# Windowed attention and two gated MLPs: decoded weights kept in HBM for the second half of the tokens

## The chip, the cores and the metric

One Trainium2 chip, one of its cores. The metric is the device time of one execution in microseconds (us). The core's engines work side by side and wait for one another through semaphores: PE (TensorE, matrix products; its weight loads are a row of their own, PEld), DVE (VectorE), ACT (ScalarE), POOL (GpSimd), and SP (SyncE), whose queue issues every DMA of this kernel in the order in which the DMAs stand there.

## What is computed

Attention over 4 sequences of 576 tokens, 8 heads of 64, each query seeing the 64 latest keys; its output, 2304 tokens by 512, goes through two gated MLPs with a hidden width of 1536:

```
x = attention(q, k, v)                                   # 2304 x 512
x = ((x @ w_val) / (1 + exp(-(x @ w_gate)))) @ w_out
x = ((x @ w_a) * (x @ w_b)) @ w_out2
```

The six weight matrices come as float64, everything else as float32.

## The kernel before

Tokens are worked in nine blocks of 256, in two halves (line 32): blocks 0 to 4, then blocks 5 to 8. A half goes through attention, then the first MLP ("phase 0"), then the second ("phase 1"). Blocks share a pass in groups of up to two, so that most products over the model dimension have 512 columns. The hidden width is cut into 12 chunks of 128, and a chunk needs three weight matrices of 128 x 512, here "a", "b" and "o". Both MLPs have 24 chunks, both halves 48 (`NW`, line 412), numbered F.

Weights reach the PE as pairs of float32r numbers, a high part and the rest, that sum to the float32 value. `load_weights` (line 237) fetches a chunk's float64 words, 512 KB a matrix, into one of three staging tiles. `decode` (line 251) makes the pair: ACT scales the low word (L259), DVE picks exponent and mantissa apart and together (L262, L266, L269, L274), POOL adds the low word (L272), ACT rounds to the high part (L279, wah/wbh/woh), POOL subtracts it to get the rest (L280, wal/wbl/wol). That is four DVE, two POOL and two ACT instructions a matrix, 144 matrices. Each half decodes all 24 chunks; the second half decodes the same words again. The pool `wts` has G + 1 = 4 places for each part, so that chunk F takes the place of chunk F - 4.

On the PE, `product` (L293) makes the gate sum gps and the value sum vps, 12 matmuls each (four chunks of the model dimension by three pairs of parts). `hidden` turns them into hh and hl (L307 to L316). `project` (L332) multiplies with "o" into acc, and `evacuate` (L349, L351) adds acc to the block's sum xacc. After the last chunk of phase 0 the sum becomes the input of phase 1: ACT writes its high part xh (L356), POOL the rest xl (L357).

Phases are cut into turns, each a group of blocks with up to three chunks; a group's projections are put out during the next turn. `step_decode` (line 416) moves the decoding on by a matrix, twice for every hidden chunk of a two-block group, once the place is free (`last_use`). The order in which each engine gets its instructions is then made by the framework's scheduler; each engine, and SP's queue, runs it in order.

Of the kernel before, what the change touches and what calls it, by code (L numbers as in the profile page):

```python
# [10 lines left out]
I32 = mybir.dt.int32  # L11
# [8 lines left out]
def tile_window_attention_gated_mlps(ctx, tc, q, k, v, w1g, w1v, w1o, w2a, w2b, w2o, out):  # L20
# [4 lines left out]
    P = 128  # L25
    NP = H // 2            # head pairs = chunks of the model dimension
    NF = DFF // P          # chunks of the hidden dimension
    G = 3                  # hidden chunks whose products are summed in PSUM
    N = 256                # tokens of a block
    TB = N // P            # 128-token tiles of a block  # L30
    # blocks that share their products over the model dimension, in two halves
    HALVES = (((0,), (1, 2), (3, 4)), ((5, 6), (7, 8)))
    W = 2 * N
    LAG = 1                # steps between the starts of two units of attention
    WIN = 64
    KW = P + WIN           # keys that a 128-query tile can see
    QSCALE = -1.0 / float(D) ** 0.5    # scores are kept negated
    MASKED = 1.0e30
# [12 lines left out]
    work = ctx.enter_context(tc.tile_pool(name="work", bufs=3))  # L51
    small = ctx.enter_context(tc.tile_pool(name="small", bufs=5))
    ps_acc = ctx.enter_context(tc.tile_pool(name="ps_acc", bufs=2, space=PSUM))
    ps_gv = ctx.enter_context(tc.tile_pool(name="ps_gv", bufs=3, space=PSUM))
    ps_at = ctx.enter_context(tc.tile_pool(name="ps_at", bufs=3, space=PSUM))
    ident = const.tile([P, P], F32, name="ident")
    make_identity(nc, ident)
    # the tensor engine's clock is up by the time that the first rows are here
    warm = ps_gv.tile([P, P], F32, tag="gv", name="warm")
    for _ in range(7):  # L60
        nc.tensor.matmul(warm, lhsT=ident, rhs=ident, start=True, stop=True)
    # queries in halves of 64, each with its window of 128 keys; the rows are those of two heads.
    # key c of the window, WIN - c tokens before the half's first query, is open to query p for
    # p + 1 <= c <= p + WIN
    mask_n = const.tile([P, P], F32, name="mask_n")
    mask_0 = const.tile([P, P], F32, name="mask_0")
    nc.gpsimd.memset(mask_n, 0.0)
    for e in range(2):
# [8 lines left out]
        )  # L77
    # the first half of a sequence has no keys before it
    nc.vector.tensor_copy(mask_0, mask_n)
    nc.vector.memset(mask_0[:, 0:WIN], MASKED)  # L80

    # ---------------------------------------------------------------- attention
    lo, hi = slice(0, D), slice(D, P)
    before, own, last = slice(0, WIN), slice(WIN, KW), slice(P, KW)
    prev = {}
    # columns: pair of heads, half of the queries, head of the pair, query; Q of the even heads
    # above zeros, of the odd heads below zeros
    qts = [const.tile([P, 2, 2, 2, WIN], F32, name=f"qt{i}") for i in range(3)]
# [12 lines left out]
    def attention(t, hq, xhi, xlo, c0):  # L101
        """Tokens [128 t, 128 t + 128) of heads [4 hq, 4 hq + 4); the result, split, goes to columns
        c0... of xhi, xlo. A generator: it stops where other work may come between."""
        starts = [j for j in range(2) if (t * P + j * WIN) % S == 0]
# [7 lines left out]

        # keys' window of the transposed K, two heads to a column; scores are kept negated
        # the first units have the banks to themselves
        p_kq, p_s = (ps_acc, "acc") if t < 4 else (ps_at, "at"), (ps_gv, "gv") if t < 2 else (ps_at, "at")
# [16 lines left out]
        prev["k", hq] = kt  # L132
        # V of the 64 keys before the tile and of its first half
        vb = work.tile([P, 4, D], F32, tag="vb", name=f"vb{t}_{hq}")
# [55 lines left out]

    # places of x: the result of the first MLP follows its input, and each group of the second
    # half one of the first half
    PLACE = {(0,): 0, (1, 2): 1, (3, 4): 2, (5, 6): 3, (7, 8): 1}
    x, done = {}, set()

    def new_x(phase, group):
        """Tiles for x of a group, in parts that sum to it; blocks have their slices."""
        w = len(group) * N
        place = PLACE[group]
        x[phase, group] = pair = tuple(  # L200
            xs.tile([P, NP, w], F32R, tag=f"x{p}{place}", name=f"x{p}{phase}_{group[0]}") for p in "hl"
        )
        for i, b in enumerate(group):
            x[phase, (b,)] = tuple(t[:, :, i * N:(i + 1) * N] for t in pair)
# [10 lines left out]
    def attention_stream(blocks):  # L215
        """The units of the blocks, a new one under way every LAG steps."""
        units = (u for blk in blocks for u in attention_units(blk))
# [13 lines left out]

    # ------------------------------------------------------------------ weights
    mats = ((w1g, w1v, w1o), (w2a, w2b, w2o))
    words = [[w.bitcast(I32) for w in m] for m in mats]    # float64: low word, high word
    staged, ready = {}, {}

# [14 lines left out]
    def decode(F):  # L251
        """Hidden chunk's weights: float64 words to float32 (rounded at the 24th bit) and on to
        float32r pairs that sum to it exactly. A generator, one matrix at a time."""
        got = {}
        for nm in "abo":
# [3 lines left out]
            nc.scalar.activation(out=low, in_=w0.bitcast(U32), func=AF.Copy, scale=2.0 ** -29)  # L259
            # the exponent: what lies below float32's range becomes 0  # L260
            ex = dec.tile([P, DM], I32, tag="ex", name="ex")
# [14 lines left out]
            )  # L276
            wh = wts.tile([P, DM], F32R, tag=f"w{nm}h", name=f"w{nm}h")
            wl = wts.tile([P, DM], F32R, tag=f"w{nm}l", name=f"w{nm}l")
            nc.scalar.activation(out=wh, in_=wf, func=AF.Copy)  # L279
            nc.gpsimd.tensor_tensor(out=wl, in0=wf, in1=wh.bitcast(F32), op=ALU.subtract)  # L280
            got[nm] = (wh, wl)
            yield
        ready[F] = got

    # --------------------------------------------------------------------- MLPs
    def product(ps, w, x):
        """ps = w^T x over the model dimension; the product of the two rests is below what the
        sums keep."""
        (wh, wl), (xh, xl) = w, x
        n = 0  # L290
        for c in range(NP):
            for a, b in ((wh, xh), (wh, xl), (wl, xh)):
                nc.tensor.matmul(  # L293
                    ps, lhsT=a[:, c * P:(c + 1) * P], rhs=b[:, c, :], start=(n == 0), stop=(n == 3 * NP - 1)
                )
                n += 1

    def hidden(phase, w, x):
# [6 lines left out]
        if phase == 0:  # L305
            # the logistic function is (1 + tanh(x / 2)) / 2; tanh is in one table set with exp
            nc.scalar.activation(out=hr, in_=gps, func=AF.Tanh, scale=0.5)  # L307
# [13 lines left out]
    def project(phase, acc, w, h, begin, end):  # L321
# [7 lines left out]
        for m, ps in enumerate(outs):  # L329
            for n, (a, b) in enumerate(pairs):  # L330
                # a start clears the written bits of the whole bank: one for both of its sums
                nc.tensor.matmul(  # L332
# [7 lines left out]
    def evacuate(phase, blk, acc, begin, end):  # L340
        """Adds the products of a few hidden chunks to what the block has so far."""
        if begin:
# [18 lines left out]

    # The turns of a phase: a block and the hidden chunks it takes. They are staggered, so that
    # chunks are done with, and others are needed, one at a time.
    # the first turns, and before each what is to be ready: blocks of attention, chunks of weights
    FIRST = (
# [8 lines left out]
    def turns(order, half, ph):  # L374
# [10 lines left out]

        if (half, ph) == (0, 0):     # as blocks come in one by one
            for _, b, fcs in FIRST:
                take((b,), len(fcs))
        elif ph == 0:
            for g in order:  # L390
                for b in g:
                    take((b,), G)
# [23 lines left out]
    def step_decode(turn):  # L416
        """One matrix of the next chunk, if the place for it is free in this turn."""
        if dec_it[0] is None:
            F = ndec[0]
            if F >= NW or (F > G and last_use[F - G - 1] >= turn):  # L420
                return False
            if nload[0] <= F:
                load_weights(F)
                nload[0] = F + 1
            dec_it[0] = decode(F)
            ndec[0] += 1
        if next(dec_it[0], "done") == "done":
            dec_it[0] = None
            F = ndec[0]
            if F < NW and nload[0] <= F:  # L430
                load_weights(F)
# [10 lines left out]
    def attend(blk=None, steps=0):  # L442
        """Puts out attention up to the end of a block, or so many steps of it."""
        while (blk is not None and blk not in done) or steps > 0:
# [11 lines left out]
    for n, (half, ph, group, fcs) in enumerate(plan):  # L456
# [14 lines left out]
        for i, fc in enumerate(fcs):  # L471
# [3 lines left out]
            if (half, ph) == (0, 1) and fc == NF - 1 and PLACE[group] == PLACE[HALVES[1][1]]:  # L475
                # the last reader of this place's x is out
                attend(HALVES[1][0][-1])
# [41 lines left out]
```

## Time and profile before

| | |
|---|---|
| median of 3 runs | 1041.39 us (1040.54 to 1041.55) |
| profiled execution, span from first to last instruction | 1039.7 us |
| busy share of the span: PE, PEld, DVE, ACT, POOL | 97%, 85%, 74%, 45%, 43% |
| DMA | 99.92 MB, 96 GB/s over the span |
| weight loads (st_a, st_b, st_o) | 144 of 512 KB, about 3.6 us each from issue to landing |

For the profiled execution the span is the time shown; the median of the runs is 1.7 us above it. A line such as "L332 PE MATMUL acc<-hh,woh 128x256 f32 x432 | 123.6, 287" is a group of instructions of line 332: output and inputs by the program's names, shape, count, busy time in us and mean duration of one in ns. Matmuls overlap, so a mean of 287 ns is not the pace; the pace is the distance between starts. Of an engine's idle time the profile names what ended it.

### The profile page before, as it was taken

The numbers are of one execution on the slowest core, as the hardware profiler recorded it, in microseconds if no ns is written. First come the engines' busy times: TensorE is split into PE (matmuls) and PEld (weight loads), VectorE is DVE, ScalarE is ACT, GpSimd is POOL, SyncE is SP. The second block draws the span as 40 slices with busy tenths as digits, with TensorE's granted clock in tenths as the row PEclk, the third lists the DMA queues.
The fourth block names the chain that finished last, engine by engine and source line by source line (L and its number), as shares of the span: only waits on it lengthen the run. The fifth ranks groups of instructions, "written<-read, shape, count | busy, mean of one in ns | idle before, by whom it ended". The sixth has DMA issues, their size and how long they took to land.

```text
span 1039.7 us, 16966 instructions
## 1 busy us (share of the span) xinstructions
PE 1007.7 (97%) x6278; PEld 886.0 (85%) x6278; DVE 766.4 (74%) x1414; ACT 467.7 (45%) x1075; POOL 447.9 (43%) x353
## 2 busy tenths in 40 slices
PE   7799999999999999999999999999999799999998
PEld 6799998989899788888888898988888788888886
DVE  5998378767868956856767696468787877787853
ACT  7887543332334665433423566333333444333320
POOL 2554055434527713524434242245454675454520
PEclk9999999999999999999999999999999999999999
DMA  8866233212312323323312372123232323232302
GB/s 203 202 174 159 57 112 102 82 61 81 102 45 78 97 76 102 102 61 102 102 61 81 100 215 63 42 81 99 84 102 81 102 74 103 86 103 82 102 1 81
DMA packets 122930, 99.92 MB, mean 96 GB/s; under 512 B 60896, under 2 KB 114400, under 8 KB 122848
## 3 DMA queue, kind: packets, MB, share of 16 engines
q1 hardware_dynamic: 122848, 98.85, 32.4%
q8 instruction: 49, 0.80, 0.3%
q14 instruction: 33, 0.27, 0.1%
HBM read 89.65 MB, written 4.72 MB: 91 GB/s over the span
## 4 chain that ended last, share of the span: by engine, by line
PE 63%; DVE 19%; POOL 7%; ACT 6%; issue 4%; DMA 1%; SPq 0%; DVEq 0%; POOLq 0%; ACTq 0%
PE acc L332 20%; PE vps L293 19%; PE gps L293 19%; DVE ex L262 5%; DVE ex L274 3%; DVE wi L269 3%; DVE xacc L351 2%; POOL wi L272 2%; POOL wal L280 2%; PE sps L146 2%; DVE hl L316 2%; POOL wol L280 1%; POOL wbl L280 1%; PE xps L182 1%; DVE wi L266 1%
## 5 line engine op out<-in xcount | busy, mean ns | idle before, releaser
L272 POOL TENSOR_TENSOR wi<-wi,low 128x512 int32<-128x512 int32 x144 | 196.6, 1365 | 107.1 <-DVE wi L269 84.0
L293 PE MATMUL gps<-xh,wah 128*128 128x512 f32 (+1 forms) x528 | 188.3, 357 | 1.9 <-ACT wah L279 1.9
L293 PE MATMUL vps<-xh,wbh 128*128 128x512 f32 (+1 forms) x528 | 186.0, 352 | 1.7 <-ACT hr L307 0.9
L293 PE MATMUL gps<-xh,wal 128*128 128x512 f32 (+1 forms) x528 | 186.0, 352 | 0.0
L293 PE MATMUL gps<-xl,wah 128*128 128x512 f32 (+1 forms) x528 | 186.0, 352 | 0.0
L293 PE MATMUL vps<-xh,wbl 128*128 128x512 f32 (+1 forms) x528 | 185.7, 352 | 0.0
L293 PE MATMUL vps<-xl,wbh 128*128 128x512 f32 (+1 forms) x528 | 185.3, 351 | 0.0
L280 POOL TENSOR_TENSOR wol<-ex,woh 128x512 fp32r<-128x512 f32 x48 | 67.1, 1397 | 179.9 <-ACT woh L279 179.9
L315 ACT ACTIVATE hh<-hr 128x512 fp32r<-128x512 f32 (+1 forms) x132 | 73.0, 553 | 150.6 <-DVE hr L311 77.4
L280 POOL TENSOR_TENSOR wal<-ex,wah 128x512 fp32r<-128x512 f32 x48 | 71.5, 1490 | 143.8 <-ACT wah L279 126.1
L332 PE MATMUL acc<-hh,woh 128*128 128x256 f32 x432 | 123.6, 287 | 5.5 <-ACT woh L279 5.3
L332 PE MATMUL acc<-hl,woh 128*128 128x256 f32 x432 | 123.7, 287 | 0.6 <-DVE hl L316 0.6
L332 PE MATMUL acc<-hh,wol 128*128 128x256 f32 x432 | 123.4, 286 | 0.0
L274 DVE SCALAR_TENSOR_TENSOR ex<-ex,wi 128x512 f32<-128x512 int32 x144 | 102.8, 714 | 16.2 <-POOL wi L272 11.2
L293 PEld LDWEIGHTS vps<-xh,wbh 128*128 128x128 f32 x528 | 100.0, 189 | 15.7 <-ACT hr L307 1.3
L280 POOL TENSOR_TENSOR wbl<-ex,wbh 128x512 fp32r<-128x512 f32 x48 | 73.0, 1520 | 92.3 <-ACT wbh L279 89.0
L293 PEld LDWEIGHTS gps<-xh,wah 128*128 128x128 f32 x528 | 100.2, 190 | 14.5 <-ACT wah L279 2.0
L293 PEld LDWEIGHTS gps<-xh,wal 128*128 128x128 f32 x528 | 100.0, 189 | 13.7
L293 PEld LDWEIGHTS vps<-xh,wbl 128*128 128x128 f32 x528 | 99.8, 189 | 13.3
L293 PEld LDWEIGHTS vps<-xl,wbh 128*128 128x128 f32 x528 | 99.8, 189 | 13.2
L293 PEld LDWEIGHTS gps<-xl,wah 128*128 128x128 f32 x528 | 100.1, 190 | 12.1
L351 DVE TENSOR_TENSOR xacc<-acc,xacc 128x512 f32<-128x512 f32 x130 | 87.3, 683 | 26.8 <-PE acc L332 26.7
(76 smaller groups left out, 2000.0 us busy)
## 6 DMA issues: line engine op xcount, KB each, us to landing
st_o<-in_moe_w_out_dram SPq DMA_DIRECT2D x48, 512.0 KB, 3.6
st_a<-in_moe_w_gate_dram SPq DMA_DIRECT2D x24, 512.0 KB, 3.6
st_b<-in_moe_w_val_dram SPq DMA_DIRECT2D x24, 512.0 KB, 3.6
st_a<-in_moe_w_a_dram SPq DMA_DIRECT2D x24, 512.0 KB, 3.5
st_b<-in_moe_w_b_dram SPq DMA_DIRECT2D x24, 512.0 KB, 3.6
out_dram<-xacc SPq DMA_DIRECT2D x18, 256.0 KB, 2.0
vb<-v SPq DMA_DIRECT2D x68, 64.0 KB, 3.1
k<-in_k_dram SPq DMA_DIRECT2D x32, 128.0 KB, 3.2
```

What stands on the lines that cost most here:

```text
L146: nc.tensor.matmul(sps[:, s, j, :], lhsT=qt[:, j, s], rhs=kt[:, j, s * WIN:s * WIN + P], start=True, stop=True)
L182: nc.tensor.matmul(xps[rows, i // 2, s * WIN:(s + 1) * WIN], lhsT=vv[:, i, :], rhs=pt[:, s, i, :], start=True, stop=True)
L262: nc.vector.tensor_scalar(out=ex, in0=w1, scalar1=(1 << 31) - 1, scalar2=20, op0=ALU.bitwise_and, op1=ALU.logical_shift_right)
L269: nc.vector.scalar_tensor_tensor(out=wi, in0=w1, scalar=-(1 << 30), in1=wi, op0=ALU.bitwise_and, op1=ALU.bitwise_or)
L272: nc.gpsimd.tensor_tensor(out=wi, in0=wi, in1=low, op=ALU.add)
L274: nc.vector.scalar_tensor_tensor(out=wf, in0=ex, scalar=897.0, in1=wi.bitcast(F32), op0=ALU.is_ge, op1=ALU.mult)
L280: nc.gpsimd.tensor_tensor(out=wl, in0=wf, in1=wh.bitcast(F32), op=ALU.subtract)
L293: nc.tensor.matmul(ps, lhsT=a[:, c * P:(c + 1) * P], rhs=b[:, c, :], start=(n == 0), stop=(n == 3 * NP - 1))
L315: nc.scalar.activation(out=hh, in_=hr, func=AF.Copy, scale=factor)
L316: nc.vector.scalar_tensor_tensor(out=hl, in0=hr, scalar=factor, in1=hh.bitcast(F32), op0=ALU.mult, op1=ALU.subtract)
L332: nc.tensor.matmul(ps, lhsT=a[:, m * P:(m + 1) * P], rhs=b, start=begin and n == 0 and (phase == 1 or m % 2 == 0), stop=end and n == 2 and ...
L351: nc.vector.tensor_tensor(out=dst, in0=ps, in1=dst, op=ALU.add)
```

## The change

Only the first half loads and decodes the words. `decode` puts both parts into one tile of 128 x 2 x 512 and adds a DMA that writes it (512 KB) to a scratch tensor in HBM, one for each matrix and chunk: 72 writes. In the second half (F >= 24) a chunk comes from `fetch`: three DMAs that read the pairs back, 72 reads of 512 KB in place of 72 loads of words. `fetch` issues a chunk's three reads in one step, where `decode` took a step for each matrix. All new DMAs stand in SP's queue. Matmuls, attention and the other instructions are the same in number; with the instructions gone the scheduler orders the engines' instructions a little differently.

```diff
+    dram = ctx.enter_context(tc.tile_pool(name="dram", bufs=1, space=bass.MemoryType.DRAM))
...
-    staged, ready = {}, {}
+    staged, ready, kept = {}, {}, {}
...
-            wh = wts.tile([P, DM], F32R, tag=f"w{nm}h", name=f"w{nm}h")
-            wl = wts.tile([P, DM], F32R, tag=f"w{nm}l", name=f"w{nm}l")
+            pair = wts.tile([P, 2, DM], F32R, tag=f"w{nm}", name=f"w{nm}")
+            wh, wl = pair[:, 0, :], pair[:, 1, :]
             nc.scalar.activation(out=wh, in_=wf, func=AF.Copy)
             nc.gpsimd.tensor_tensor(out=wl, in0=wf, in1=wh.bitcast(F32), op=ALU.subtract)
             got[nm] = (wh, wl)
+            kept[F, nm] = dram.tile([P, 2, DM], F32, tag=f"k{nm}{F}", name=f"k{nm}{F}")
+            nc.sync.dma_start(out=kept[F, nm], in_=pair.bitcast(F32))
             yield
         ready[F] = got
...
+    def fetch(F):
+        got = {}
+        for nm in "abo":
+            pair = wts.tile([P, 2, DM], F32R, tag=f"w{nm}", name=f"w{nm}")
+            nc.sync.dma_start(out=pair.bitcast(F32), in_=kept[F - 2 * NF, nm])
+            got[nm] = (pair[:, 0, :], pair[:, 1, :])
+        ready[F] = got
+        yield
...
-            if nload[0] <= F:
+            if F < 2 * NF and nload[0] <= F:
                 load_weights(F)
                 nload[0] = F + 1
-            dec_it[0] = decode(F)
+            dec_it[0] = decode(F) if F < 2 * NF else fetch(F)
...
-            if F < NW and nload[0] <= F:
+            if F < 2 * NF and nload[0] <= F:
                 load_weights(F)
```

The order of instructions at three places follows. The changed kernel's line numbers are up to 13 higher; ka, kb, ko are the scratch tensors, and wa, wb, wo are the pairs.

SP's queue in the opening, from the V copies of the seventh unit of attention on (k, q, v are attention's loads, vb copies of V rows, st_ the weight words). Before:

```order
L139 DMA vb_0_409<-v_0_283 64x256
L135 DMA vb_0_409<-v_0_397 64x256
L110 DMA v_0_513<-in_v_dram 64x4x64 x2
L245 DMA st_b<-in_moe_w_val_dram 128x4x256
L110 DMA k_1_780<-in_k_dram 128x4x64
L110 DMA q_1_782<-in_q_dram 128x4x64
L135 DMA vb_1_466<-v_1_454 64x256
L139 DMA vb_1_466<-v_1_340 64x256
L243 DMA st_o<-in_moe_w_out_dram 128x1024
L110 DMA v_1_669<-in_v_dram 64x4x64 x2
L110 DMA k_0_839<-in_k_dram 128x4x64
```

Now:

```order
L140 DMA vb_0_411<-v_0_285 64x256
L284 DMA ka_549<-wa 128x1024
L136 DMA vb_0_411<-v_0_399 64x256
L111 DMA v_0_515<-in_v_dram 64x4x64 x2
L246 DMA st_b<-in_moe_w_val_dram 128x4x256
L111 DMA k_1_788<-in_k_dram 128x4x64
L284 DMA kb_563<-wb 128x1024
L136 DMA vb_1_468<-v_1_456 64x256
L140 DMA vb_1_468<-v_1_342 64x256
L244 DMA st_o<-in_moe_w_out_dram 128x1024
L111 DMA v_1_677<-in_v_dram 64x4x64 x2
L111 DMA q_1_790<-in_q_dram 128x4x64
```

The first chunk's writes ka and kb stand among attention's loads and ahead of the next chunk's words; ko follows two rows later.

SP's queue in the second half, some chunks into phase 0. The bracket names what a DMA waits for: DMAHW is an earlier DMA of the same semaphore, eight places ahead. Before:

```order
L245 DMA st_a<-in_moe_w_a_dram 128x4x256 [waits DMAHW0_49,DVE_49]
L245 DMA st_b<-in_moe_w_b_dram 128x4x256 [waits DMAHW1_49,DVE_49]
L243 DMA st_o<-in_moe_w_out_dram 128x1024 [waits DMAHW2_49,DVE_49]
L245 DMA st_a<-in_moe_w_a_dram 128x4x256 [waits DMAHW3_49,DVE_49,Activation_49]
L245 DMA st_b<-in_moe_w_b_dram 128x4x256 [waits DMAHW4_49,DVE_49]
```

Now:

```order
L293 DMA wa<-ka_3108 128x1024 [waits DMAHW7_49,PE_49]
L293 DMA wb<-kb_3122 128x1024 [waits DMAHW0_49,PE_49]
L293 DMA wo<-ko_2828 128x1024 [waits DMAHW1_49,PE_49]
L293 DMA wa<-ka_3335 128x1024 [waits DMAHW2_49,PE_49]
L293 DMA wb<-kb_3422 128x1024 [waits DMAHW3_49,PE_49]
```

The queue no longer waits for the decoding on DVE but for the PE to have done with the place that a read fills.

POOL where the second half goes from phase 0 to phase 1 (xl is the input of phase 1, xl_7 of blocks 7 and 8, xl_5 of 5 and 6). Before:

```order
L357 TENSOR_TENSOR xl_7_9265<-xacc_7817,xh_7_9264 128x2x256
L272 TENSOR_TENSOR wi<-wi,low 128x512
L357 TENSOR_TENSOR xl_7_9265<-xacc_7817,xh_7_9264 128x2x256
L280 TENSOR_TENSOR wbl<-ex,wbh 128x512
L272 TENSOR_TENSOR wi<-wi,low 128x512
L280 TENSOR_TENSOR wol<-ex,woh 128x512
L357 TENSOR_TENSOR xl_7_9265<-xacc_7957,xh_7_9264 128x2x256
L272 TENSOR_TENSOR wi<-wi,low 128x512
L357 TENSOR_TENSOR xl_7_9265<-xacc_7957,xh_7_9264 128x2x256
```

Now:

```order
L126 COPY kt_1_7240<-kt_1_7054 128x2x64
L370 TENSOR_TENSOR xl_7_8845<-xacc_7729,xh_7_8844 128x2x256 x2
L370 TENSOR_TENSOR xl_7_8845<-xacc_7869,xh_7_8844 128x2x256 x2
L370 TENSOR_TENSOR xl_5_8995<-xacc_7379,xh_5_8994 128x2x256 x2
L370 TENSOR_TENSOR xl_5_8995<-xacc_7589,xh_5_8994 128x2x256 x2
```

The decoding that stood between the pieces of xl is gone. On the PE, what follows the last projection of phase 0 also moved. From the end of blocks 5 and 6 up to the first use of xl_5, before:

```order
L332 MATMUL acc_9462<-hl,woh 128x256
L332 MATMUL acc_9462<-hh,wol 128x256
L293 MATMUL gps<-xh_5_9453,wah 128x512
L293 MATMUL vps<-xh_5_9453,wbh 128x512
L293 MATMUL gps<-xl_5_9454,wah 128x512
```

Now:

```order
L345 MATMUL acc_9003<-hh,wo 128x256
L345 MATMUL acc_9073<-wo,hh 128x512 x2
L345 MATMUL acc_9073<-wo,hl 128x512
L306 MATMUL gps<-xh_5_8994,wa 128x512
L306 MATMUL vps<-xh_5_8994,wb 128x512
L306 MATMUL gps<-xh_5_8994,wa 128x512
L345 MATMUL acc_9074<-wo,hh 128x512 x2
L345 MATMUL acc_9074<-wo,hl 128x512
L345 MATMUL acc_9123<-wo,hh 128x512 x2
L345 MATMUL acc_9123<-wo,hl 128x512
L306 MATMUL gps<-xl_5_8995,wa 128x512
```

Twelve matmuls now stand between the last one of phase 0 and the first that reads xl_5; before there were two, and ten that read xl_7 had been put ahead of the last projection's final three.

## Rows read from the trace of the kernel before

**Rows 1.** The page: busy time, share of the span and instructions of each engine.
```profile
PE 1007.7 (97%) x6278; PEld 886.0 (85%) x6278; DVE 766.4 (74%) x1414; ACT 467.7 (45%) x1075; POOL 447.9 (43%) x353
```

**Rows 2.** Windows: length, busy us (instructions) of PE, PEld, DVE, ACT, POOL; clock, DMA share, GB/s.
```profile
0.00:100.00 100.00, 84.96 (x811) 78.72 (x812) 85.56 (x287) 80.88 (x266) 47.55 (x55) 0.98 0.74 187
590.00:650.00 60.00, 57.54 (x495) 52.89 (x494) 46.86 (x128) 38.42 (x118) 21.57 (x18) 1.00 0.44 128
650.00:820.00 170.00, 169.14 (x1032) 151.39 (x1031) 125.83 (x178) 64.11 (x109) 76.47 (x55) 1.00 0.27 84
820.00:840.00 20.00, 14.71 (x89) 13.86 (x88) 15.69 (x19) 7.53 (x12) 15.71 (x13) 0.83 0.25 80
840.00:1000.00 160.00, 159.54 (x706) 131.29 (x705) 127.58 (x172) 62.73 (x106) 84.27 (x59) 1.00 0.27 86
```

**Rows 3.** Waits of the PE, 600 to 1040 us: total us, times, longest.
```profile
PE acc L332 <- ACT woh L279: 5.3, 1, 5.3
PE tps L172 <- DVE nmax L155: 2.4, 2, 1.6
PE vps L293 <- ACT hr L307: 0.9, 1, 0.9
PE vps L293 <- ACT hr L310: 0.3, 1, 0.3
PE acc L332 <- DVE xacc L351: 0.2, 1, 0.2
```

**Rows 4.** The chain that ended last, 820 to 834 us: start, us, what.
```profile
824.58 1.58 POOL wbl L280
826.19 1.47 DVE ex L262
...
828.18 0.69 DVE ex L274
...
828.95 0.64 ACT woh L279
```

**Rows 5.** Windows around that wait, columns as in rows 2.
```profile
829.60:835.50 5.90, 5.89 (x26) 5.71 (x27) 3.91 (x5) 2.39 (x4) 5.84 (x5) 0.50 0.38 139
835.50:841.40 5.90, 5.90 (x38) 5.32 (x38) 5.40 (x6) 1.87 (x3) 5.19 (x4) 1.00 0.06 19
```

**Rows 6.** The chain over the whole span: three runs of matmuls, start, us, what.
```profile
232.20 4.31 PE acc L332 x36
...
868.19 4.08 PE acc L332 x18
...
1001.53 4.08 PE acc L332 x18
```

**Rows 7.** Groups of DVE and POOL, 590 to 1040 us.
```profile
L351 DVE TENSOR_TENSOR xacc<-acc,xacc 128x512 f32<-128x512 f32 x64 | 43.1, 683 | 12.7 <-PE acc L332 12.5
```
```profile
L357 POOL TENSOR_TENSOR xl<-xacc,xh 128x512 fp32r<-128x512 f32 x8 | 11.8, 1478 | 3.5 <-ACT xh L356 3.5
```

**Rows 8.** ACT in order of time at 829 us: start, us, what.
```profile
829.49 0.63 ACT L356 ACTIVATE xh<-xacc 128x512 fp32r<-128x512 f32 x1
```

**Rows 9.** The page: DMA issues, count, KB each, median us to landing.
```profile
st_o<-in_moe_w_out_dram SPq DMA_DIRECT2D x48, 512.0 KB, 3.6
...
out_dram<-xacc SPq DMA_DIRECT2D x18, 256.0 KB, 2.0
```

**Rows 10.** Windows of the opening, columns as in rows 2.
```profile
30.00:40.00 10.00, 9.95 (x92) 9.23 (x89) 8.30 (x24) 9.00 (x30) 6.60 (x6) 0.83 0.77 176
40.00:50.00 10.00, 7.57 (x70) 6.78 (x70) 9.97 (x32) 7.93 (x27) 5.23 (x6) 1.00 0.97 236
50.00:60.00 10.00, 9.13 (x96) 8.79 (x97) 9.53 (x31) 8.63 (x30) 5.19 (x5) 1.00 0.75 200
```

**Rows 11.** The chain that ended last, in the opening: start, us, what.
```profile
39.00 5.11 DMA st_o<-in_moe_w_out_dram
44.18 5.66 DMA st_a<-in_moe_w_gate_dram
```

**Rows 12.** SP's queue in order of time in the opening: start, us, what.
```profile
37.76 0.51 SPq L135 DMA_DIRECT2D vb<-v  x1
```

**Rows 13.** DVE in order of time: the first use of the two loads of rows 11.
```profile
50.92 0.43 DVE L266 TENSOR_SCALAR wi<-st_o 128x512 int32<-128x512 int32 x1
```
```profile
57.12 0.94 DVE L266 TENSOR_SCALAR wi<-st_a 128x512 int32<-128x512 int32 x1
```

## The prediction

> **What bounds the kernel now.** I read the page's first part, then a table of windows, then the PE's waits. The page has the PE busy for 97% of the span and no other engine above 74% [rows 1]. Busy time alone would not prove the PE full, because matmuls overlap; the pace does. A run of 18 matmuls of 512 columns takes 4.08 us at 868 us, in the middle of the decoding, and 4.08 us at 1001 us, after it has ended: 0.227 us each. A run of 36 with 256 columns takes 4.31 us: 0.120 us each [rows 6]. So the decoding does not slow a matmul down; it can only make the PE wait. The windows show where it does. In the opening 100 us the PE is busy for 84.96, with DVE (85.56) and ACT (80.88) as full as it. In the second half of the tokens, from about 590 us on, it loses 2.5 us of 60, then 0.9 of 170, then 5.3 of 20, then 0.5 of 160 [rows 2]. Only the second half loses work by this change, so what it can win lies in these few places: the PE's waits from 600 us on sum to 9.1 us, and 5.3 of them are one wait [rows 3]. The 72 decodings that go are a large part of what DVE and POOL do there, but in nearly all of this stretch they run beside matmuls.
>
> **The change part by part.**
>
> *The long wait, -8.0 us.* At 824.2 us the PE comes to the first projection that needs a woh still being decoded. The chain has POOL finishing wbl (1.58), DVE's ex (1.47), DVE's ex again (0.69) and ACT's woh (0.64), each behind the one before [rows 4]: a decoding in a row, held up where DVE and POOL must also carry the sums into phase 1. The PE waits 5.3 us [rows 3]. Then it pays again: after that idle time its granted clock is 0.50, the lower level of 1.2 GHz, in 829.6 to 835.5, and 1.00 after it [rows 5]. Of the 26 matmuls that start there the last starts at the very end; the others, two of 512 columns and 23 of 256, would take 2 x 0.227 + 23 x 0.120 = 3.2 us at the upper level, and the stretch took 5.9, so the half clock cost about 2.7. After the change that woh is read from HBM. A read of 512 KB should land in about the 3.6 us of a load of 512 KB [rows 9]. When can it start? Every read waits for the PE's last use of the place it fills, and in the new order the tightest of the 72 (some of the "o" reads) have 72 matmuls of 512 columns between that last use and their own first use: 72 x 0.227 = 16.3 us, against 3.6. Reads behind one another in SP's queue wait for PE work that lies in the same order, so the queue does not eat that margin. I take the whole 8.0; its lower bound is treated as a rival.
>
> *Small waits, -1.4 us.* vps twice waits for ACT's hr, 0.9 and 0.3, and acc once for DVE's xacc, 0.2 [rows 3]: results that stand behind decoding on ACT or DVE. With half the DVE work of this stretch gone I let all of it go; the ends are 0 and 1.4.
>
> *Attention of the second half, -1.2 us.* In 590 to 650 us the PE waits 2.4 us for DVE's scores, nmax [rows 3], while chunks are also decoded. Attention's own chain through DVE and ACT remains, so I take half; ends 0 and 2.4.
>
> *The turn into phase 1, +0.5 us.* With the long wait gone, what is late next is the new input of phase 1. After the last matmul of a block's projection come DVE's xacc (0.68), ACT's xh (0.63) and POOL's xl (1.48), each twice, for the two halves of the model dimension [rows 7, 8]. The first half's xacc runs beside the last six matmuls, so the first xl is there 0.63 + 1.48 = 2.1 us after the end; the second follows 1.48 later and is first read ten matmuls after the first. For blocks 7 and 8 the new order has 24 matmuls of 256 and two of 512 columns as cover before the first reader, 24 x 0.120 + 2 x 0.227 = 3.3 us; for blocks 5 and 6 it has 12 of 512, 2.7 us. Both are enough, by 1.2 and 0.6. If a reader needed the whole chain, 0.68 + 0.63 + 2 x 1.48 = 4.3 us, the PE would wait 1.0 + 1.6. Between 0 and 2.6 I take 0.5, near the lower end, because DVE and POOL have no other work there.
>
> *72 writes in the first half, +2.0 us, all in the opening.* From 100 us to 590 us the PE hardly ever waits and the DMA engines have most of their time free, so a write there hides behind matmuls. Each write waits for POOL's wl; but the next load of words behind it in the queue waits for DVE's ex of the matrix after, which comes no earlier, because the single ex tile is read by that same POOL instruction. So the wait adds nothing to SP's queue. What is left is the opening. No row shows a write of 512 KB. The nearest are the 256 KB output at 2.0 us [rows 9], so at most 4.0, and the rate at a DMA share of 0.97, 236 GB/s [rows 10], which gives 0.524 MB / 236 GB/s = 2.2 us of all the DMA engines. By the order, two chunks' writes, six, fall into 30 to 60 us: 6 x 2.2 = 13.3 us. The free share there is 2.3 + 0.3 + 2.5 = 5.1 us [rows 10]. So transfers fall up to 8.2 us behind by 60 us. The weight words can bear most of it: st_o is issued at 39.00, landed at 44.1 and is first read at 50.92; st_a landed at 49.84 and is read at 57.12 [rows 11, 13]; 6.8 and 7.3 us in hand. Attention's loads have less: SP issues back to back there, 0.51 us for a DMA [rows 12], and three more issues ahead of st_a put it back by 1.5 us. The ends are -1 (the scheduler's new order may by chance fit better) and 8.2 + 1.5 = 9.7; nearest is the slip of the issues, 1.5 us, and I add a little for the queue: 2.0.
>
> *Nothing else.* The reads move as many bytes as the loads they replace. ACT's, DVE's and POOL's free time in the second half is worth nothing beyond the waits above, since the PE is the bound.
>
> Sum: -8.0 - 1.4 - 1.2 + 0.5 + 2.0 = -8.1. The profiled execution spans 1039.7 us, so 1031.6; the median of the runs lies 1.7 us above that span, so **1033.3 us**.
>
> **The rivals.**
>
> *A: the long wait is refilled.* The PE may now arrive early at phase 1 and find xl missing for a whole chain: 4.3 us in place of the 0.5 allowed. For it: in the trace POOL's xl shares these microseconds with decoding, and margins of 1.2 and 0.6 are thin. Against: with decoding gone both engines are free when the sum is ready. 1033.3 + 3.8 = 1037.1.
>
> *B: the writes choke the opening.* It is bound by DVE and ACT, which live on loads; DMA is at 0.97 in 40 to 50 us, and a load is already on the chain there [rows 10, 11]. If each of the nine writes of the first three chunks puts all its 2.2 us on the path, that is 20 us: 1041.4 - 10.6 + 0.5 + 20 = 1051.3. It decides the sign once the opening loses more than 10.1 us; up to 12.2 the result would still be within 0.2%, which is about what a measurement of this kernel can tell from no change. Against it stand the 7 us in hand and the free DMA time after 60 us.
>
> *C: the reads come late.* If SP stands at a read whose place is not free and the next turn's reads are stuck behind it, the PE waits for a landing. The price is 3.6 us a time; once for each of eight turns in the two phases it would be 29 us, and 1060. The 16.3 us of cover speaks against it; fewer late reads would end near no change.
>
> *D: the matmuls themselves are held up by decoding.* Then the pace would change, not the waits. The weight loads are busy for 131.29 of the 160 us from 840 on, 82% [rows 2]; if all of the missing 18% were the decoding's doing, some 430 us would shrink by 77 us, to about 964. The Trainium skill's page "Perfetto Trace Analysis" (Identifying the Most-Contended Engine) says that matmul busy time is a poor measure of headroom and that LDWEIGHTS busy share should be used instead; by that rule the PE would have this 18% to give. The trace disagrees here: the pace is 0.227 us with decoding and without it [rows 6].
>
> That the change does not do what it says is excluded by the order: half of the decode instructions are gone from ACT, DVE and POOL, and the PE has as many matmuls as before.
>
> **How the numbers follow.** The forecast has 0.64, A 0.15, B 0.15, C 0.04, D 0.02. The forecast's own spread runs from 1041.4 - 12.8 = 1028.6 (both attention waits go, the opening gains 1) to about 1037 (the opening costs 6). B spreads from the choked 1051 down; of its 0.15 I put 0.08 within 0.2% and 0.07 slower; C is split 0.01, 0.01 and 0.02. Faster by over 0.2%: 0.64 + 0.15 + 0.02 + 0.01 = 0.82; within: 0.09; slower: 0.09. A range from 1028 to 1040.5 holds the forecast and A and leaves out most of B, C and D, about 0.2.
>
> **What would show it.** Right: in the PE's waits no acc waiting for the weights, a granted clock of 1.00 from 600 to 1000 us, PE busy over 99% in the twenty microseconds at the turn into phase 1, reads landing in 3 to 4 us, and in the first 100 us a PE busy time lower by about 2 us. Wrong: a PE that waits for a DMA wo, wa or wb (C), for POOL's xl (A), a first 100 us that is short of PE work by over 6 us more (B), or a pace other than 0.227 us for 512 columns (D).

## The result, and the profile after

The changed kernel takes **1030.91 us** (median of 4 runs, 1029.41 to 1031.98) beside 1041.03 (1040.54 to 1041.55): a ratio of 0.9899, 95% interval [0.9885, 0.9913]. The forecast was 1033.3 with 1028 to 1040.5. Below it is seen that the mechanism lay where it was expected, at the turn into phase 1, but that one of its steps named the wrong object and another the wrong cause.

The profiled execution spans 1030.2 us (its run: 1031.98). The page's busy times, which answer to [rows 1]: DVE has lost 223 us of work and POOL 206, and the PE has the same 6278 matmuls.

```profile
PE 1008.6 (98%) x6278; PEld 887.0 (86%) x6278; DVE 543.7 (53%) x1126; ACT 382.8 (37%) x931; POOL 242.0 (23%) x209
```

The windows, same columns as [rows 2] and answering to it:

```profile
0.00:100.00 100.00, 86.91 (x784) 79.96 (x785) 84.01 (x279) 81.25 (x265) 46.39 (x54) 0.93 0.88 241
...
590.00:650.00 60.00, 60.00 (x509) 55.16 (x508) 28.85 (x108) 31.83 (x108) 1.18 (x4) 1.00 0.39 116
650.00:820.00 170.00, 170.00 (x1042) 152.68 (x1041) 44.61 (x70) 31.31 (x57) 2.53 (x2) 1.00 0.31 100
820.00:840.00 20.00, 19.73 (x121) 17.35 (x121) 6.04 (x9) 7.35 (x12) 7.71 (x6) 1.00 0.33 106
840.00:1000.00 160.00, 160.00 (x707) 132.55 (x706) 41.20 (x60) 28.16 (x46) 0.00 (x0) 1.00 0.24 79
```

From 590 to 1000 us the PE is busy but for 0.27 us, at a granted clock of 1.00 (at the turn for 98.7% of the twenty microseconds, where the prediction asked for over 99). Of the waits of [rows 3] one row is left (all of the PE's waits, 600 to 1040 us):

```profile
PE acc L345 <- DVE xacc L364: 0.4, 2, 0.2
```

The first window reads better than it is: the PE is busy for longer (86.91 against 84.96 us) but has put out fewer matmuls (784 against 811), at a mean clock of 0.93 against 0.98. The opening around 30 to 60 us, to be laid beside [rows 10]:

```profile
30.00:40.00 10.00, 9.84 (x79) 9.18 (x80) 7.16 (x25) 7.68 (x26) 4.13 (x5) 0.69 0.85 239
40.00:50.00 10.00, 9.29 (x96) 8.29 (x95) 10.00 (x29) 8.80 (x30) 6.19 (x6) 1.00 1.02 288
50.00:60.00 10.00, 8.02 (x65) 7.54 (x63) 9.41 (x33) 7.41 (x25) 4.35 (x5) 0.83 0.99 261
```

Over the whole run the medians of the writes of 512 KB are 2.6 to 3.1 us to landing and those of the reads 3.3 to 4.0, beside 3.6 for a load [rows 9]; the lowest and the highest row (page, DMA issues: count, KB, median us to landing):

```profile
ka<-wa SPq DMA_DIRECT2D x24, 512.0 KB, 2.6
...
wo<-ko SPq DMA_DIRECT2D x24, 512.0 KB, 4.0
```

The pace is what it was, 4.08 us for 18 matmuls of 512 columns (chain that ended last), as in [rows 6]:

```profile
909.08 4.08 PE acc L345 x18
```

For a balance I took, for every matmul, the distance to the next one's start less the pace of its shape (0.227 us for 512 columns, 0.120 for 256, and so on for attention's), and summed this per stretch: the PE time lost. The columns are stretches in us from the start of the span, the rows are kernels; those below after_again are the experiments. The turn into phase 1 of the second half lies in 820 to 860. Differences of the totals agree with those of the spans within 0.2 us.

```
us lost in        0-100 100-320 320-440 440-600 600-660 660-820 820-860  860-   sum   span
before             20.6    1.4     5.1     0.6     4.1     1.4     8.2    1.6   43.0  1039.7
after              22.5    2.1     5.5     0.6     1.6     0.1     0.9    0.2   33.5  1030.2
after_again        20.0    2.0     5.4     0.6     1.7     0.1     0.9    0.2   30.8  1027.6
e1_writes_only     20.5    1.9     5.4     0.6     4.1     2.2     7.6    1.6   43.9  1040.6
e2_read_two        22.2    2.0     5.5     0.6     4.1     2.2     1.2    2.1   39.8  1036.6
e2b_all_but_two    20.5    1.9     5.4     0.6     1.7     0.1     0.9    0.2   31.3  1027.9
e3_banks           20.6    1.4     5.2     0.6     4.1     1.3     8.7    1.3   43.2  1040.0
e5_sums_first      22.0    1.6     5.2     0.6     4.1     1.4     3.0   10.7   48.5  1045.2
e7_after_sums      20.6    1.9     4.3     0.6     1.7     0.4     0.6    0.2   30.3  1027.0
e8_six_decoded     20.5    1.9     5.5     0.6     1.6     0.1     6.3    0.2   36.8  1033.7
e9_two_held        22.5    2.1     5.4     0.6     1.7     0.1     0.9    0.2   33.4  1030.1
e10_one_held       22.1    1.6     5.2     0.6     4.1     1.4     5.0    7.4   47.3  1044.1
```

### The profile page after: what moved, and what is told of

Its sections match the earlier page's. It is cut to its first block, busy times and chain, and to the rows that moved or that the text cites. A ratio compares the mean times of both kernels' runs of the same rounds, so it can differ in the third digit from the quotient of the medians.

```text
span 1030.2 us, 16412 instructions
## 1 busy us (share of the span) xinstructions
PE 1008.6 (98%) x6278; PEld 887.0 (86%) x6278; DVE 543.7 (53%) x1126; ACT 382.8 (37%) x931; POOL 242.0 (23%) x209
## 4 chain that ended last, share of the span: by engine, by line
PE 84%; DVE 9%; ACT 3%; issue 2%; POOL 2%; DMA 1%; SPq 0%; POOLq 0%; DVEq 0%; ACTq 0%
PE acc L345 26%; PE gps L306 26%; PE vps L306 25%; PE sps L147 2%; PE xps L183 2%; PE tps L173 1%; DVE ex L263 1%; DVE wi L270 1%; DVE ex L275 1%; DVE hl L329 1%; ACT pr L161 1%; PE kqps L120 1%; DVE wi L267 1%; DVE xacc L364 1%; POOL wi L273 1%
## 5 line engine op out<-in xcount | busy, mean ns | idle before, releaser
L306 PE MATMUL gps<-xh,wa 128*128 128x512 f32 (+1 forms) x1056 | 303.8, 355 | 1.0 <-ACT wa L280 1.0
L306 PE MATMUL vps<-xh,wb 128*128 128x512 f32 (+1 forms) x1056 | 301.1, 352 | 0.5 <-ACT wb L280 0.5
L306 PEld LDWEIGHTS gps<-xh,wa 128*128 128x128 f32 x1056 | 190.9, 190 | 27.6 <-ACT wa L280 1.3
L306 PEld LDWEIGHTS vps<-xh,wb 128*128 128x128 f32 x1056 | 190.2, 190 | 27.1 <-ACT wb L280 0.7
L306 PE MATMUL gps<-xl,wa 128*128 128x512 f32 (+1 forms) x528 | 186.7, 354 | 0.8 <-DVE xl L187 0.7
L306 PE MATMUL vps<-xl,wb 128*128 128x512 f32 (+1 forms) x528 | 185.8, 352 | 0.0
L345 PE MATMUL acc<-hh,wo 128*128 128x256 f32 x864 | 166.0, 284 | 1.0 <-DVE xacc L364 1.0
L345 PEld LDWEIGHTS acc<-hh,wo 128*128 128x128 f32 x864 | 138.2, 191 | 2.8 <-DVE xacc L364 1.1
L345 PE MATMUL acc<-wo,hh 128*128 128x512 f32 x432 | 133.5, 391 | 2.4 <-DVE xacc L364 1.6
L345 PE MATMUL acc<-hl,wo 128*128 128x256 f32 x432 | 122.5, 284 | 1.2 <-DVE hl L329 1.2
```

The costliest lines, as they stand in the source:

```text
L306: nc.tensor.matmul(ps, lhsT=a[:, c * P:(c + 1) * P], rhs=b[:, c, :], start=(n == 0), stop=(n == 3 * NP - 1))
L345: nc.tensor.matmul(ps, lhsT=a[:, m * P:(m + 1) * P], rhs=b, start=begin and n == 0 and (phase == 1 or m % 2 == 0), stop=end and n == 2 and ...
```

## The experiments

The long wait of [rows 3] is put down to woh. DVE's queue before it, in order of time (kernel before: start, us, line, what), suggested something else. The sum xacc of 828.78 ends at 829.46, and the PE goes on at 829.60 [rows 5]; ahead of that sum stand four pieces of a decoding:

```profile
823.87 0.43 DVE L266 TENSOR_SCALAR wi<-st_o 128x512 int32<-128x512 int32 x1
824.33 0.69 DVE L269 SCALAR_TENSOR_TENSOR wi<-st_o,wi 128x512 int32<-128x512 int32 x1
824.94 0.68 DVE L308 SCALAR_TENSOR_TENSOR hr<-hr,vps 128x512 f32<-128x512 f32 x1
826.19 1.47 DVE L262 TENSOR_SCALAR ex<-st_o 128x512 int32<-128x512 int32 x1 [0.57 <-POOL wbl L280]
827.58 0.68 DVE L316 SCALAR_TENSOR_TENSOR hl<-hr,hh 128x512 fp32r<-128x512 f32 x1
828.18 0.68 DVE L274 SCALAR_TENSOR_TENSOR ex<-ex,wi 128x512 f32<-128x512 int32 x1
828.78 0.68 DVE L351 TENSOR_TENSOR xacc<-acc,xacc 128x512 f32<-128x512 f32 x1
```

In this kernel acc is a tile in PSUM, into which the PE writes its sums; a new acc takes the bank of an older one once DVE has added that one to xacc. The Trainium skill's page "Perfetto Trace Analysis" (Identifying Dependency Chains) says to read the semaphores that an instruction waits on from its own text. In the compiled order that matmul waits for DVE and for ACT: for DVE's emptying of the PSUM bank that the new acc takes, and for ACT's hh. The profile had named what ended last before the PE went on: woh, at 829.59.

**e1_writes_only, e2_read_two, e2b_all_but_two, e3_banks**, beside 21 runs of the kernel before with a median of 1041.48 us. e1 keeps the writes and decodes in the second half again (the main line of the edit; it also loads the words of all chunks again):

```diff
-            dec_it[0] = decode(F) if F < 2 * NF else fetch(F)
+            dec_it[0] = decode(F)
...
```

> The 72 writes of the changed kernel stay, but the second half loads and decodes the words again, as the kernel before. My theory: the writes cost what the opening pays for them and nothing later, so this run is the kernel before plus 0 to 2 us, 1041 to 1043, with the waits of about 8 us at 820 to 840 us unchanged. Rival (writes are dear, and the reading back wins more than the 8.1 us I gave it): 1045 or more. Rival (the gain comes from the new layout of the pairs or the new order in the opening, not from decoding that is gone): 1036 or less.

Measured: 1043.22 us, ratio 1.0019 [1.0011, 1.0028]: the theory, at its upper end, with the wait at the turn still there (7.6 us lost). 72 writes, with the pair in one tile, cost 1.7 us by the medians, and none of it in the first 100 us: 20.5 are lost there beside 20.6 before, at a DMA share of 0.89. Its profiled run lost 0.9 us more than before: 0.5 at 100 to 320, 0.3 at 320 to 440 and 0.8 at 660 to 820 us, while 0.6 were won at the turn.

e2 and e2b are the changed kernel with another choice of the chunks that are read back: `READ` is (36, 37) in e2, and in e2b 24 to 47 without these two; only what is read back is written.

```diff
-            dec_it[0] = decode(F) if F < 2 * NF else fetch(F)
+            dec_it[0] = fetch(F) if F in READ else decode(F)
...
```

> Only the two chunks 36 and 37, whose decoding falls into the turn from phase 0 to phase 1 of the second half, are read back (6 writes, 6 reads); the other 22 chunks of the second half are decoded again. Theory (the long wait comes from decoding that stands in the queues of DVE and POOL at the turn): the wait of 5.3 us and the slow clock behind it go, 6 to 8 us faster than before, 1033 to 1035. Rival (it is the volume of decoding, spread over the second half): 2 of 24 chunks are worth a twelfth of 10 us, under 1 us, 1040 or more. A third outcome, 1036 to 1039: chunk 38 or 35 takes the place of 37 in the queue and part of the wait stays.

> The counterpart: of the second half all chunks are read back but 36 and 37, which are loaded and decoded again (66 writes, 66 reads). Theory: the decoding that stands at the turn is still there, so a wait of several us at 820 to 840 us stays; only the small waits and attention's go, and the writes cost up to 2: 1037 to 1040. Rival (volume): 22 of 24 parts of the gain, about 1032.

Measured: e2 1036.68, ratio 0.9959 [0.9946, 0.9973]; e2b 1031.49, ratio 0.9902 [0.9888, 0.9915]. In e2 the long wait is gone with two chunks of 24 (the window at the turn):

```profile
820.00:840.00 20.00, 19.73 (x125) 17.48 (x123) 9.55 (x14) 7.23 (x12) 9.91 (x8) 1.00 0.17 53
```

By its ratio the run gains 4.3 us and not 6 to 8. Its time lies in the range of the third outcome, but not for that reason: hardly any of the long wait stayed (1.2 us lost at 820 to 860 against 0.9). The turn does give 7.0 back, of the 7.3 that the whole change gives there; 0.8 and 0.5 are lost again at 660 to 820 and behind 860 us, and 1.0 at 100 to 440, as in all kernels here with the pair in one tile (0.8 to 1.1, but for e7); its first 100 us had a clock of 0.93, of which more below.

e2b missed: with chunks 36 and 37 decoded the wait did not come back. Its DVE queue shows why: the last decoding there is over at 808.1 us (DVE in order of time), and the turn finds DVE without any:

```profile
807.41 0.69 DVE L276 SCALAR_TENSOR_TENSOR ex<-ex,wi 128x512 f32<-128x512 int32 x1 [1.18 <-POOL wi L274]
```

The wait needs decoding that lags into the turn, not two particular chunks; e8 below tests that.

e3 gives the last phase-0 projection of block 5 other PSUM banks (the expectation speaks of blocks 5 and 6; `blk == HALVES[1][0][0]` is block 5 alone, the first that has to wait):

```diff
-        acc = [ps_acc.tile([P, 2, N], F32, tag="acc", name=f"acc{j}") for j in range(2)]
+        p, tag = (ps_at, "at") if ph == 0 and end and blk == HALVES[1][0][0] else (ps_acc, "acc")
+        acc = [p.tile([P, 2, N], F32, tag=tag, name=f"acc{j}") for j in range(2)]
```

> The kernel before, with all decoding; only the last projections of phase 0 in blocks 5 and 6 take their accumulators from attention's PSUM banks, which are free by then, so that they don't wait for the bank that DVE's evacuation (xacc, in queue behind the decoding of chunk 37) holds. My prediction's reading (the PE waits for the decoded weights woh): the wait of 5.3 us stays at the same matmul. Second reading (it waits for the bank that DVE empties late): that matmul no longer waits; what is late next is the input of phase 1, which hangs on the same late evacuations, so 0 to 3 us faster, 1038 to 1041. Third reading (the bank alone, nothing behind it): 8 us faster, 1033.

Measured: 1041.92, ratio 1.0007 [0.9998, 1.0016]: no gain, so nothing of the 0 to 3 us of the second reading. But it decides what the PE waited for. Up to there both kernels put out the same matmuls in the same order. The one that stood until 829.61 now starts at 824.17, without a wait; twelve matmuls later the same projection waits for the next chunk's hh, then for its hl (PE in order of time):

```profile
824.17 0.28 PE L332 MATMUL acc<-hh,woh 128*128 128x256 f32 x1
...
826.32 0.38 PE L332 MATMUL acc<-hh,woh 128*128 128x256 f32 x1 [0.55 <-ACT hh L315]
828.32 0.39 PE L332 MATMUL acc<-hl,woh 128*128 128x256 f32 x1 [1.62 <-DVE hl L316]
```

while the same woh ends, as before, only at 829.59 (ACT):

```profile
828.96 0.63 ACT L279 ACTIVATE woh<-ex 128x512 fp32r<-128x512 f32 x1 [0.87 <-DVE ex L274]
```

So it never needed that woh (a weight of phase 1, chunk 37): it ran 5.4 us ahead of it. It needed the bank; with the bank given, it needs hh and hl, and phase 1 then needs xl, which all hang on results in DVE's queue. The loss at the turn is no smaller, 8.7 us against 8.2, now in several pieces, of which xl is one (PE's waits):

```profile
PE gps L293 <- POOL xl L357: 1.5, 1, 1.5
```

**e5_sums_first, e8_six_decoded, e7_after_sums, after_again**, beside 9 runs of the kernel before with a median of 1040.71 us. e5 is the kernel before, with an order written by hand: `issue_after` queues decoding on DVE behind the last sum put out so far. The same edit on the changed kernel, for the first half's blocks, is e7:

```diff
+                ev = nc.vector.tensor_tensor(out=dst, in0=ps, in1=dst, op=ALU.add)
+                if phase == 0 and end and blk in HALVES[1][0] + HALVES[1][1]:
+                    first[0] = ev.ins
...
+        with tc.issue_after(first[0]) if first[0] else nullcontext():
+            more = next(dec_it[0], "done")
```

> The kernel before with all of its decoding and no scratch; only the order in DVE's queue changes: at the turn of the second half into phase 1, a matrix's decoding is queued behind the sums (xacc) that were traced before it, so that it no longer stands ahead of them. Theory (it is the place of the decoding in DVE's queue, not its amount): the wait of 5.3 us and the slow clock behind it go, 5 to 8 us faster than before, 1033.5 to 1036.5. Rival (DVE and POOL simply have too much to do there): the decoding comes late instead, the PE waits for wa, wb or wo of chunks 37 and 38 by as much, 1040 or more.

Measured: 1046.78, ratio 1.0056 [1.0043, 1.0068], so the rival. At the turn 5.2 us come back (8.2 to 3.0) and 9.1 are lost behind it. The PE's waits, 600 us on, now for what the held decoding delays:

```profile
PE acc L333 <- DVE xacc L352: 5.7, 7, 1.9
PE vps L294 <- ACT hr L311: 3.2, 3, 1.8
```

DVE is busy for 132.47 of the 160 us behind the turn. That its 28 idle us leave too little room to catch up without standing in the way of the next sums is my reading; the waits for xacc and hr above fit it.

e8 is the changed kernel with 33 to 38 left out of `READ`, so that these are decoded again.

> Of the second half's 24 chunks 18 are read back, and 33 to 38 are loaded and decoded again, which puts the same decoding into the same places of DVE's queue at the turn as in the kernel before (with 36 and 37 alone decoded, it had been done ten microseconds ahead of the turn). Theory (place in the queue): the long wait is back, 820 to 840 us loses several us of PE time, 1036 to 1039. Rival (amount): a quarter of the decoding brings back a quarter of the 10 us, 1033 to 1034.

Measured: 1036.56, ratio 0.9956 [0.9944, 0.9969]. The wait is back, 4.6 us, with the profile again blaming a weight (PE's waits; the window at the turn) while, as before, a sum xacc in DVE's queue ends 0.14 us before the PE goes on (825.80 and 825.94), and 820 to 860 us loses 6.3 where the changed kernel loses 0.9, with all other stretches as in that kernel. Six chunks of 24 bring back 5.4 of its 7.3 us, not a quarter:

```profile
PE acc L347 <- ACT wo L281: 4.6, 1, 4.6
```

```profile
820.00:840.00 20.00, 15.44 (x90) 13.97 (x89) 17.45 (x22) 8.02 (x14) 15.97 (x11) 0.91 0.23 81
```

> The changed kernel, and in the first half, where all chunks still are decoded, the same edit of DVE's queue: at the turn into phase 1 decoding is queued behind the sums. In the changed kernel the PE loses 4 to 5 us between 320 and 380 us. If the place in the queue is what matters there too, 2 to 4 us of these go and the run is faster than the changed kernel: 1027 to 1029. Rival (the decoding held back makes weights late after that turn, since in the first half DVE also carries attention of the next blocks): 1030 or more.

Measured: 1028.63, ratio 0.9881 [0.9867, 0.9894], the lowest of all, 1.2 us under after_again on the same chip, with intervals that overlap: in time the two are not told apart. In the first half, too, the sums stand behind decoding at the turn. The edit frees the turn (56.83 us of PE work in 320 to 380 us in the changed kernel, 60.00 here), and then 1.7 us of wait for hl comes at 405 us (windows; the loss at 320 to 440 goes from 5.5 to 4.3 only, since a stretch of half clock follows that wait):

```profile
320.00:380.00 60.00, 60.00 (x350) 52.35 (x350) 51.67 (x101) 37.93 (x95) 38.66 (x31) 1.00 0.54 167
380.00:590.00 210.00, 208.30 (x1150) 176.74 (x1149) 134.82 (x248) 80.44 (x182) 67.82 (x54) 0.99 0.46 152
```

> The changed kernel again, for the spread of its runs. The prediction gave the writes of the opening 2.0 us. But with the writes and the old order of the opening no PE time was lost there, and without any write in the opening but with the new order 1.7 us were. If this is the granted clock and not the order, the runs fall into two groups, about 1029.5 at a mean clock of 0.998 and about 1031.9 at 0.993, and a profile at 0.998 loses as little PE time in the first 100 us (20.5 us) as the kernel before. If it is the order, a profile at 0.998 loses 2 us more than that all the same.

Measured: 1029.88 (1029.33 to 1031.46), ratio 0.9899 [0.9884, 0.9914]; the profiled run had the clock at 0.998. Its first 100 us:

```profile
0.00:100.00 100.00, 85.87 (x816) 78.29 (x817) 86.32 (x291) 81.45 (x269) 47.49 (x55) 0.98 0.90 249
```

816 matmuls, with the same writes and the same order as in the first profile's 784. And e5, which has no write and, up to the turn, the very program of before, lost 22.0 us there at a clock of 0.93:

```profile
0.00:100.00 100.00, 87.29 (x789) 80.33 (x790) 84.27 (x281) 81.04 (x265) 46.35 (x54) 0.93 0.72 183
```

In one and the same program after_again is 0.5 us ahead of the first profile at matmul 140 (24.4 against 24.9 us) and 2.7 us ahead at matmul 780 (96.9 against 99.6); the stretch at half clock lies between. So the 2 us come with the granted clock, whatever the kernel.

**e9_two_held, e10_one_held**, beside 9 runs of the kernel before with a median of 1040.93 us, limit what is held back, e9 in e7 (up to chunk 13, as below) and e10 in e5 (up to chunk 36, with 37 in place of 14):

```diff
-        with tc.issue_after(first[0]) if first[0] else nullcontext():
+        with tc.issue_after(first[0]) if first[0] and ndec[0] <= 14 else nullcontext():
```

> As e7_after_sums, but only the chunks 12 and 13, the first two of phase 1, are held behind the sums at the first half's turn; from chunk 14 on the decoding stands where it likes. In e7_after_sums the 5 us at the turn had gone, but 1.9 us of wait and 1.7 of slow clock had come at 405 us, where a result (hl) stood in DVE's queue behind decoding that had been held back. If that wait came of too much decoding being held back, it goes and the run gains 2 to 3.5 us on e7_after_sums: 1025 to 1027. If the debt is there whichever chunks are held, it shows up in another place: 1028 to 1029.5.

> As e5_sums_first (all decoding kept, no scratch), but only chunk 36 is held behind the sums at the second half's turn; chunk 37 stands where the scheduler puts it. e5_sums_first took the long wait at the turn away and paid 10 us between 860 and 960 us for decoding that came late. If that was too much held back, this run keeps the turn free and pays less: 1034 to 1038. If the second half simply carries more decoding after the turn than DVE can do beside the rest (the debt is moved, not paid), the PE loses as much in all as in the kernel before, or more, at the turn or later: 1040 to 1047.

Measured: e9 1031.27, ratio 0.9901 [0.9886, 0.9917], the changed kernel again, above both ranges (5.4 us lost at 320 to 440; of its two waits for xacc the first fell from 0.9 to 0.2 us and the second grew from 1.4 to 2.2). e10 1044.31, ratio 1.0033 [1.0021, 1.0046]: 5.0 us lost at the turn and 7.4 behind it, more than the 8.2 and 1.6 of before. Both fall to the second reading, the debt, e9 by its waits and not by its time. No order tried here pays it in the second half; less work does.

## Why the prediction was right or wrong

*Where the time is.* Right. The whole of the net gain lies behind 600 us; the matmuls keep their pace, so D is out.

*The long wait, -8.0.* Right in size and place, wrong in its object. The step "the PE comes to the first projection that needs a woh still being decoded" fails: e3 shows the projection starting 5.4 us before that woh is done. What was late was the emptying of a bank, and behind it hh, hl and xl, which all hang on results that stood in DVE's queue behind decoding that lagged. The 16.3 us of cover that I worked out for the reads was therefore an answer to a question that this wait had not asked; it did hold, as no PE wait names a read. Stretch 820 to 860 us: 8.2 lost before, 0.9 after.

*The turn into phase 1, +0.5.* Is part of those 0.9; waits for xacc make 0.4 of it. Rival A asked for a whole chain of 4.3. It fell, because DVE and POOL are idle when the sum comes: from 650 to 1000 us POOL has 10 us of work and DVE 92 of 350.

*Small waits, -1.4, and attention, -1.2.* Both terms mis-sized by half, toward the same side: -2.7 (660 to 820 us: 1.4 to 0.1; behind 860: 1.6 to 0.2, of which [rows 3] lists only part, the rest being gaps of under 0.5 us) and -2.4 (600 to 660: 4.1 to 1.7). "Attention's own chain through DVE and ACT remains, so I take half" failed: with no decoding in DVE's queue the wait for nmax went entirely.

*72 writes in the opening, +2.0.* The number met the first profile (22.5 against 20.6) by accident, and the step fails. The sign named for it, a PE busy time lower by about 2 us, did not come: it was 86.91 against 84.96. Writes in the opening cost nothing: 20.0 to 20.6 us are lost with them (after_again, e1, e2b, e7, e8) as without (before, e3), at a DMA share of up to 0.90. The writes there did take longer than the 4.0 us allowed for them: the twelve of the first 100 us in after_again landed in 2.6 to 5.5 us, with a median of 4.3, and the PE lost nothing by it. My term took the slip of st_a in SP's queue, 1.5 us, as the price although rows 11 and 13 had shown 7 us in hand for it; that attention's loads had less was said without a row. So B is out. What the writes or the joint tile do cost is some 0.9 us at 100 to 440 us, which I had set to nothing because the PE "hardly ever waits" there; it loses 6.5 us there in the kernel before. e2, with 6 writes, pays it as e1 does with 72, which points to the tile; no run took it apart.

The sum for after_again, whose opening had the clock of before: -0.6 + 0.6 + 0.3 - 2.4 - 1.3 - 7.3 - 1.4 = -12.1, the difference of the spans (1027.6 - 1039.7). For the first profile it is -9.5, which is the forecast's -8.1, less 2.6 for the small waits and attention and 0.1 in the opening, plus 0.2 at the turn and 1.1 at 100 to 440 us; its 2.0 for the opening stands there for a clock that falls in some runs. So the time of 1030.91 lies within 2.4 us of the forecast partly by luck: with the opening at the clock of the profile before, the kernel gains 12.1 us where 8.1 were forecast.

## What to carry to other kernels

An engine at 74% can still hold up one at 97%, at the one place where it lags and its queue carries both kinds of work; the price is read from that place. Two chunks of 24 taken out (e2) gave back 7.0 of the 7.3 us there, and the other 22 (e2b) all of them: either way DVE had no decoding ahead of the sums when they came. What counts is the lag on arrival, not which work is left out. When a wait is put down to what ended last, look at what the waiting instruction itself waits for before costing the cure. Reordering the queue only moved the debt where DVE was 83% busy behind the place (e5, e10).

## What was not expected of the hardware

**The clock of the opening.** The changed kernel took 1029.3 to 1029.9 us in the five runs with a mean clock of 0.998 and 1031.5 to 1032.0 in the three with 0.993. The kernel before splits alike: 1039.8 to 1041.6 us in its runs with 0.993 or more, 1041.7 to 1042.5 in those with 0.991 or less. In the first profile (0.993) the granted clock was at the lower level, 1.2 GHz, for most of 25 to 36 us, after 25 us in which the PE had been busy for 17.86 (windows), and once more, for a shorter time, at 50 to 60 us (0.83, above):

```profile
0.00:25.00 25.00, 17.86 (x143) 15.05 (x145) 14.56 (x78) 19.64 (x70) 6.96 (x21) 1.00 0.82 206
...
25.00:36.00 11.00, 9.30 (x66) 8.30 (x65) 9.31 (x31) 8.91 (x32) 4.36 (x4) 0.54 0.76 209
```

The shorter stretch of this kind in [rows 10] cost nothing: e1 and e3 had a clock of 1.00 throughout the first 100 us and lost as much there (20.5 and 20.6). That DVE and ACT bound the opening would explain it; no run tests that. The two stretches together go with 2 us. Why a run gets the one or the other is open.

**A decoding step on DVE waits for POOL's instruction to end.** The same instruction ex<-st (128 x 512) took 0.43 us at 799.59 with POOL idle and 1.52 at 819.36 with POOL at work, in the kernel before (DVE, then POOL in order of time):

```profile
799.59 0.43 DVE L262 TENSOR_SCALAR ex<-st_a 128x512 int32<-128x512 int32 x1 [0.26 <-POOL wol L280]
819.36 1.52 DVE L262 TENSOR_SCALAR ex<-st_b 128x512 int32<-128x512 int32 x1
```

```profile
818.85 1.74 POOL L357 TENSOR_TENSOR xl<-xacc,xh 128x512 fp32r<-128x512 f32 x1
820.55 1.47 POOL L272 TENSOR_TENSOR wi<-wi,low 128x512 int32<-128x512 int32 x1
```

Over its 144 instructions the median is 0.42 without overlap (25 of them) and 1.50 with it (119). What counts is which starts first: 99 started while POOL was busy with L272 or L357, and each ended 0.28 to 0.29 us after that instruction of POOL's, as 820.88 does after 820.59 above; 12 started ahead of L272 and took 0.42 as if alone. DVE's sums xacc (L351), which read PSUM, took 0.68 either way. The Trainium skill's page "Trainium Architecture — The Big Picture" (What this means for kernel authors) says that of the engines only DVE and GpSimd contend for SBUF, by an exclusive lock on a shared pair of ports; these rows agree. So decoding, whose DVE steps lie among its own POOL steps, costs DVE more than its 2.2 us a matrix (0.42 + 0.43 + 0.69 + 0.69): 3.2 on the average of the 144. That may be part of why it lagged at the turn; no run takes it away by itself. Without decoding beside it xl takes 1.29 us on POOL in place of 1.48 [rows 7].
